# A new written-out order for the first 18 pairs of an attention and feed-forward kernel

## The chip, the cores and the metric

The kernel runs on one core of a Trainium2 chip. The metric is the time of one execution in microseconds (us), as the median of the runs shown. The profile is that of one execution; its span runs from the first to the last instruction of the program, and the execution's own time is a little longer.

Five engines work side by side, each through its own instructions in order: PE (TensorE, matmuls), ACT (ScalarE), DVE (VectorE), POOL (GpSimd) and SP (SyncE, which here only issues DMAs). They wait for each other by semaphores.

## The reference

Cosine attention over 8 batches, 12 heads, 448 positions of 64 numbers, then a feed-forward layer over all 3584 rows:

```python
q_n = q / (norm(q) + 1e-6);  k_n = k / (norm(k) + 1e-6)
attn = softmax(q_n @ k_n.T / tau)               # per head, tau = 0.1
x = (attn @ v).transpose(0, 2, 1, 3).reshape(3584, 768)
h = x @ w_in                                    # 768 x 2048
out = (h * clip(h + 3, 0, 6) / 6) @ w_out       # 2048 x 768
```

## The kernel before, in words

**Pairs and items.** Two heads make a pair; there are 48 pairs, six to a batch. The inputs come as items: item 2d and 2d+1 hold q and k of pairs 2d and 2d+1 (448 KB each; from item 14 on k comes first). Everything is computed in bf16 after the norms. PE does the matmuls of both halves of the work, so attention of later batches runs between the feed-forward units of earlier ones.

**Order by hand.** The instructions of all engines are issued in the order in which the program calls its helper functions. Up to pair 17 this order is a text, `PLAN` (L21 to L58), read word by word by `run` (L960); each word is a function and its arguments. Behind it, a loop over pairs 18 to 47 (L999) has an order of its own. Within one engine the order of the words is the order of execution. The words are:

- `LQ.j` loads item j on SP's queue (L189); it takes over the buffer of item j - 7, so it waits for that item's scaling. `LV.d` loads v of two pairs by four DMAs on SP (L201); its buffer was that of d - 3, so it waits for the casts of that one's two pairs.
- `SQ.j.e.c.n` squares n columns of item j on engine e, which is a (ACT), p (POOL) or v (DVE) (L211). `RE.j` sums the squares on DVE (L228). `NO.d` makes 1/(norm + eps) of items 2d and 2d+1: by four small ACT operations, or, with a `v` behind it, by two of ACT and two of DVE (L246 to L262). `NM.j.e` scales item j by it (L266), on POOL unless `v` is given. Items 0 and 1 are squared, summed and scaled in pieces; a number behind the word says which half.
- `TR.j` transposes item j on PE, seven small matmuls into a PSUM bank (L314); from item 14 on `XD.j` does it by a DMA on SP (L325). `CQ.i`, `CK.i` and `CS.i` copy queries and keys of pair i out of it (L352 to L388).
- `SC.i.g` computes scores of group g (of four) of pair i on PE (L395), `EX.i.g` their exps on ACT (L428). `VC.i.e` casts v of pair i (L285), `VA.i.g` multiplies exps by v on PE, eight small matmuls (L453). Up to pair 5, scores go to two double banks, so a group waits for the exps of the group two before; behind `OPEN` (L926) to a ring of six banks that all PE results share.
- `FI.i` divides by the sums on DVE (L473). `BK.i` transposes the result back on PE and `CX.i` copies it into the input of the feed-forward layer on DVE (L490, L498); `XP` and `XB` do both by DMA.
- `W` asks for the next eighth of the weights, by a DMA on POOL's queue that also casts them to bf16 (L908). Four pieces make w_in: the first two hold its columns 0 to 1023, the next two the rest. Four make w_out.
- `U` runs the next unit of the feed-forward layer on PE. A unit of the first weight matmul is six matmuls of 448 columns (`mm1_unit`, L561, matmuls at L567); it needs `CX` of the batch's six pairs, the weight pieces of its columns, and a bank of the ring. `UA` and `UV` run the ACT and DVE operations that empty a unit's bank (L576, L582). The order has 30 such units (16 of batch 0, 14 of batch 1), then 6 of the second weight matmul of batch 0 (`mm2_unit`, L607, sixteen matmuls each at L614). Later units take sums of blocks so that seven products do for eight (`product_unit`, L721, matmuls at L740).
- `DP.n` runs n fillers of 248 columns on PE, `D.n` n fillers of 512 columns: matmuls of a zero tile whose results nobody reads (L914 to L924).
- `GL` and `WS` copy and add blocks on DVE.

Each helper names what must have been issued ahead of it (`needs`, L167), and the waits between engines follow from the buffers that it reads and writes. For the first unit that is

```python
def mm1_unit(b, fc):
    needs(*(("CX", i) for i in range(b * HP, (b + 1) * HP)))
    assert len(weights) <= 6 - 2 * (2 * fc // FCN)
```

that is, two pieces of the weights must have been asked for ahead of units 1 to 8 of a batch (`fc` 0 to 7), four ahead of units 9 to 16.

Of the kernel before, what the change touches and what calls it, by code (L numbers as in the profile page):

```python
# [18 lines left out]
ORDER = "111111111111111111111111111111222222"  # L19

PLAN = [  # L21
    "LQ.1 DP.5 SQ.1.a.11.3 SQ.1.p.4.3 DP.1 SQ.1.a.0.4 LQ.0 SQ.0.p.8.6 DP.2 DP.4 LQ.3 LQ.2 SQ.1.v.7.4 RE.1.1",
    "SQ.0.a.0.6 RE.1.0 NO.0.1 LQ.5 LQ.4 SQ.0.v.6.2 DP.6 NM.1.p.0 D.10 RE.0.1 DP.3 NM.1.p.1 RE.0.0 DP.8 NO.0.0",
    "SQ.3.a.0.7 LV.0 DP.2 SQ.2.a.0.7 NM.0.p.0 RE.3 RE.2 NM.0.p.1 TR.1.Y DP.2 TR.0.Z CK.0.v DP.4 SQ.4.p.0.7 CQ.0.v",
    "SQ.5.a.0.7 LQ.6 NO.1 LV.1 LQ.7 SC.0.0.0 SC.0.1.1 DP.5 DP.3 CQ.1.v EX.0.0 RE.5 RE.4 NM.3.p SC.0.2.0 CK.1.v DP.3",
    "EX.0.1 DP.3 EX.0.2 NM.2.v DP.3 SC.0.3.1 TR.3.Y LQ.8 NO.2 EX.0.3 DP.3 SC.1.0.0 TR.2.Z EX.1.0 VC.0.v SC.1.1.1 DP.2",
    "EX.1.1 VA.0.0 CK.2.v VC.1.v VC.3.v NM.4.p NM.5.p VA.0.1 LQ.9 SC.1.2.0 SQ.6.a.0.7 LQ.11 DP.5 DP.2 SC.1.3.1 EX.1.2",
    "CQ.2.v LQ.10 LV.2 VA.0.2 VA.0.3 DP.3 SC.2.0.0 DP.2 EX.1.3 CK.3.v SC.2.1.1 EX.2.0 TR.4.Y SC.2.2.0 SQ.7.p.0.7",
    "EX.2.1 RE.6 FI.0 RE.7 LV.3 VA.1.0 SQ.8.p.0.7 SC.2.3.1 CQ.3.v VC.2.v CQ.5.v VA.1.1 EX.2.2 SC.3.0.0 EX.2.3 VA.1.2",
    "NO.3 RE.8 SC.3.1.1 CQ.4.v EX.3.0 DP.2 DP.4 EX.3.1 VA.1.3 TR.5.Z SC.3.2.0 W SQ.9.p.0.7 EX.3.2 FI.1 CK.4.v BK.0.Y",  # L30
    "VA.2.0 SC.3.3.1 RE.9 LV.4 EX.3.3 NO.4 VA.2.1 VA.2.2 VA.2.3 SC.4.0.0 EX.4.0 NM.6.p DP.2 SC.4.1.1 SQ.10.p.0.7 W",
    "SQ.11.p.0.7 EX.4.1 CX.0.v TR.6.Y CK.5.v FI.2 CQ.7.v VA.3.0 BK.2.Z RE.10 SC.4.2.0 EX.4.2 NM.7.p CQ.6.v VA.3.1",
    "SC.4.3.1 DP.2 EX.4.3 CX.2.v SC.5.0.0 RE.11 VA.3.2 EX.5.0 SC.5.1.1 VA.3.3 VC.4.p SC.5.2.0 FI.3 VC.5.p EX.5.1",
    "BK.1.Y TR.7.Z SC.5.3.1 CX.1.v CK.6.v CK.7.v VA.4.0 EX.5.2 DP.2 CS.7.v EX.5.3 BK.3.Y VA.4.1 LQ.12 CS.6.v OPEN",
    "DP.2 CX.3.v NO.5 SC.6.0 VA.4.2 VA.4.3 SC.6.1 SC.6.2 EX.6.0 NM.8.p FI.4 EX.6.1 EX.6.2 SC.6.3 TR.8 BK.4 VA.5.0",
    "CX.4.v VA.5.1 CQ.8.v SC.7.0 VA.5.2 EX.6.3 NM.9.p CQ.9.v VC.6.p VA.5.3 SC.7.1 FI.5 EX.7.0 SC.7.2 TR.9 SC.7.3",
    "NM.10.p CK.8.v VA.6.0 EX.7.1 EX.7.2 VC.8.p CS.8.v W BK.5 SQ.12.p.0.7 LQ.13 VA.6.1 VA.6.2 SC.8.0 EX.7.3 CS.9.v",
    "VA.6.3 CK.9.v DP.1 EX.8.0 CX.5.v SC.8.1 SC.8.2 VC.7.p FI.6 LQ.15 EX.8.1 U UA SQ.13.a.0.7 LV.5 U TR.10 EX.8.2 UA",
    "U RE.13 U SC.8.3 UV UA CQ.10.v VA.7.0 W RE.12 UV CQ.11.a UV UA NO.6 U EX.8.3 VA.7.1 VA.7.2 UV VC.9.p VA.7.3",
    "NM.11.p SC.9.0 FI.7 NM.12.p UA SC.9.1 UV EX.9.0 U VA.8.0 SC.9.2 EX.9.1 VC.10.p UA SC.9.3 TR.11 UV NM.13.p",  # L40
    "CS.11.v XP.6 VA.8.1 LQ.14 EX.9.2 SQ.15.a.0.7 VA.8.2 U EX.9.3 CK.11.v CK.10.v VA.8.3 SC.10.0 TR.12 U CS.10.v FI.8",
    "UA UV VA.9.0 SC.10.1 LQ.17 EX.10.0 SQ.14.p.0.7 CQ.12.v CQ.13.v SC.10.2 UA VA.9.1 LQ.19 VA.9.2 EX.10.1 LQ.16",
    "VA.9.3 LV.6 W UV SC.10.3 EX.10.2 U SC.11.0 FI.9 EX.10.3 SC.11.1 U UA EX.11.0 LV.7 EX.11.1 UV UA SC.11.2 RE.15",
    "BK.8 LQ.18 CX.8.v U VA.10.0 U VA.10.1 UA EX.11.2 UV UV RE.14 SC.11.3 UA BK.9 VA.10.2 VA.10.3 FI.10 EX.11.3 TR.13",
    "NO.7 CK.13.v CS.13.v CX.9.a U UV CK.12.a VC.11.p W VA.11.0 U SC.12.0 CS.12.v VA.11.1 VA.11.2 UA BK.10 VA.11.3 UV",
    "UA NM.15.p UV EX.12.0 CX.10.v SC.12.1 EX.12.1 SC.12.2 FI.11 U EX.12.2 BK.11 SC.12.3 UA NM.14.p SQ.16.p.0.6 U UA",
    "CX.11.v UV U SC.13.0 SQ.17.p.0.7 XD.14 UV RE.17 EX.12.3 VC.12.p EX.13.0 SQ.16.a.6.1 U UA RE.16 VC.15.p U VA.12.0",
    "UV XD.15 UA U UA UA UV SC.13.1 SQ.19.p.0.7 VC.13.p SC.13.2 UV EX.13.1 LQ.21 U VA.12.1 VA.12.2 UA UV RE.19",
    "VA.12.3 EX.13.2 UV NO.8 W U SC.13.3 NM.16.p CK.15.v CK.14.v U UA UA SQ.18.a.0.7 EX.13.3 U SC.14.0 FI.12 UA",
    "VA.13.0 VC.14.p CS.14.v UV VA.13.1 UV EX.14.0 UV U SC.14.1 SC.14.2 VA.13.2 VA.13.3 UA EX.14.1 UV U W SC.14.3",  # L50
    "FI.13 U VA.14.0 NM.17.p UA EX.14.2 UA VA.14.1 EX.14.3 XD.17 U UV VA.14.2 RE.18 SC.15.0 SC.15.1 UA UV EX.15.0 U",
    "XD.16 EX.15.1 UA UV VA.14.3 SC.15.2 U UA SC.15.3 EX.15.2 FI.14 NO.9 LV.8 VA.15.0 LV.9 UV CK.16.v UV EX.15.3 U",
    "SQ.21.p.0.7 VA.15.1 RE.21 CS.16.v LQ.20 SC.16.0 LQ.22 SC.16.1 UA VC.16.p SC.16.2 VC.17.p VA.15.2 EX.16.0 VA.15.3",
    "XP.12 NM.18.v CK.17.v XD.18 U EX.16.1 SQ.20.a.0.7 NM.19.p FI.15 WS.6 U UV XD.19 SC.16.3 RE.20 GL.0 WS.1 WS.7.0",
    "EX.16.2 U VA.16.0 UA VA.16.1 LV.11 EX.16.3 SC.17.0 UV VC.19.p SC.17.1 SC.17.2 SQ.22.v.0.7 VA.16.2 LQ.23 EX.17.0",
    "VA.16.3 EX.17.1 LV.10 U SC.17.3 XP.14 NO.10 FI.16 NM.20.p CK.18.v U CK.19.v WS.7.1 WS.y3 XB.16 EX.17.2 UV UA",
    "VA.17.0 VC.18.p EX.17.3 CS.18.v WS.y4.0",
]  # L58


# [1037 lines left out]
```

## Time and profile before

| | |
|---|---|
| time, median of 3 runs | 406.7 us (406.68 to 407.45) |
| profiled execution | 404.91 us, span 403.1 us |
| clock granted to TensorE | 1.0 throughout |
| instructions | 9619 |
| moved by DMA | 65.32 MB, 162 GB/s on average |
| q or k loads | 48 of 448 KB, 4.4 to 4.9 us from issue to landing (median) |
| weight pieces | 8 of 768 KB, 9.2 to 10.2 us (median) |

How to read it: the page gives each engine's busy time and its share of the span; then the span in 40 slices; the DMA queues; the chain of waits, which follows the work back from the last instruction to whatever released it; and groups of instructions by line, engine and tile, with `out<-in`, the number, the busy time and the mean duration. A timeline has one line for a run of like instructions: start, length, engine, line, operation, tiles, number, and in brackets the idle time ahead of it with what ended it. "Pitch" below is the time from one start to the next of the same engine; it is shorter than an instruction's duration, since they overlap by a tenth of a microsecond or so.

### The profile page before, as it was taken

What the parts mean: (1) busy time and instruction counts of PE and PEld (TensorE: products, weight loads), DVE (VectorE), ACT (ScalarE), POOL (GpSimd) and SP (SyncE); (2) the same over time, 40 slices, a digit from 0 to 9 for tenths busy, and PEclk for the clock granted to TensorE, in tenths of its full rate; (3) what the DMA queues carried; (4) which work ended last, traced back from release to release, by engine and by line L of the source; (5) the groups of instructions that cost most, each with busy time, mean ns of one, the idle gap of its engine ahead of it and who ended that gap; (6) DMA issues with size and microseconds to landing.
All of it is one profiled execution on the core that took longest, in us unless ns stands there. A gap on an engine that the chain in (4) does not pass through costs nothing.

```text
span 403.1 us, 9619 instructions
## 1 busy us (share of the span) xinstructions
PE 395.5 (98%) x3696; PEld 234.3 (58%) x3696; DVE 286.4 (71%) x503; ACT 278.3 (69%) x609; POOL 234.0 (58%) x228
## 2 busy tenths in 40 slices
...
GB/s 289 281 254 257 216 247 230 156 125 230 187 213 220 139 128 228 171 222 130 180 216 212 152 130 164 182 192 145 192 154 76 112 46 67 41 79 21 26 73 99
DMA packets 91566, 65.32 MB, mean 162 GB/s; under 512 B 56064, under 2 KB 89984, under 8 KB 91520
## 3 DMA queue, kind: packets, MB, share of 16 engines
q1 hardware_dynamic: 87408, 58.02, 62.8%
q0 software_dynamic: 3712, 6.29, 9.0%
...
q10 hardware_dynamic: 400, 0.39, 0.3%
...
## 4 chain that ended last, share of the span: by engine, by line
PE 94%; DVE 3%; DMA 1%; ACT 0%; issue 0%; DVEq 0%; ACTq 0%
PE M L567 24%; PE M L740 17%; PE PV L462 13%; PE Y L567 6%; PE M L422 6%; PE Z L567 5%; PE Y L740 4%; PE Z L740 4%; PE M L614 3%; PE M L820 2%; PE Z L422 2%; PE PV L922 2%; PE Z L820 1%; PE Y L422 1%; DVE n L238 1%; PE SC L422 1%
## 5 line engine op out<-in xcount | busy, mean ns | idle before, releaser
L440 ACT ACTIVATE at<-M 128x448 bf16<-128x448 f32 x200 | 99.9, 568 | 16.4 <-PE M L422 14.4
L567 PE MATMUL M<-xT,w_in_sb 128*128 128x448 bf16 x522 | 110.8, 352 | 0.0
L567 PEld LDWEIGHTS <-w_in_sb 128*128 128x128 bf16 x768 | 72.0, 98 | 62.6 <-issue 2.8
L274 POOL TENSOR_TENSOR nrm<-big,r 128x896 bf16<-128x896 f32 (+1 forms) x48 | 79.5, 1662 | 26.1 <-ACT r L262 19.3
L576 ACT ACTIVATE u<-M,bias 128x448 bf16<-128x448 f32 x87 | 57.0, 655 | 25.2 <-PE M L567 24.8
L582 DVE SCALAR_TENSOR_TENSOR gT<-u,M 128x448 bf16<-128x448 bf16 x76 | 46.7, 618 | 36.8 <-ACT u L576 36.3
L226 POOL TENSOR_TENSOR big<-big 128x896 f32<-128x896 f32 (+3 forms) x39 | 63.9, 1641 | 10.9 <-DMA big<-in_k_dram 5.7
L462 PEld LDWEIGHTS <-at 128*128 128x128 bf16 (+1 forms) x1536 | 54.9, 97 | 22.8 <-issue 13.5
L462 PE MATMUL PV<-vx,at 128*128 128x65 bf16 (+1 forms) x1536 | 64.3, 194 | 0.2 <-DVE on L483 0.2
L238 DVE TENSOR_REDUCE n<-big 128x14 f32<-128x896 f32 (+1 forms) x50 | 51.7, 1041 | 5.6 <-ACT big L224 4.6
L379 POOL COPY km<-tT 64x128 bf16<-64x128 bf16 x34 | 12.8, 376 | 58.1 <-DMA tT<-nrm 45.1
L769 POOL TENSOR_TENSOR big<-big 128x384 f32<-128x384 f32 x11 | 11.8, 1076 | 54.6 <-ACT big L788 54.5
L740 PEld LDWEIGHTS <-gT 128*128 128x128 bf16 x288 | 27.8, 98 | 20.0 <-DVE gT L718 0.6
L740 PE MATMUL M<-w_out_sb,gT 128*128 128x384 bf16 x208 | 37.9, 326 | 0.1
L440 ACT ACTIVATE at<-Z 128x448 bf16<-128x448 f32 x49 | 27.7, 565 | 9.9 <-PE M L422 7.3
L483 DVE TENSOR_TENSOR on<-PV,rc 128x512 bf16<-128x512 f32 x48 | 33.2, 691 | 1.7
L293 POOL CAST vx<-big 128x512 bf16<-128x512 f32 x44 | 33.2, 757 | 1.2 <-DMA big<-in_v_dram 1.1
L422 PE MATMUL M<-tT,kz 64*128 64x448 bf16 (+1 forms) x175 | 31.6, 351 | 0.0
L740 PEld LDWEIGHTS <-gs 128*128 128x128 bf16 x224 | 21.5, 98 | 14.8 <-DVE gs L718 0.4
L567 PE MATMUL Y<-xT,w_in_sb 128*128 128x448 bf16 x132 | 28.6, 352 | 0.0
L440 ACT ACTIVATE at<-Y 128x448 bf16<-128x448 f32 x45 | 25.7, 570 | 3.1 <-PE Z L422 1.7
L740 PE MATMUL M<-w_sum,gs 128*128 128x384 bf16 x144 | 26.3, 326 | 0.0
...
## 6 DMA issues: line engine op xcount, KB each, us to landing
...
w_in_sb<-in_moe_w_in_dram POOLq DMA_DIRECT2D x4, 768.0 KB, 10.2
w_out_sb<-in_moe_w_out_dram POOLq DMA_DIRECT2D x4, 768.0 KB, 9.2
tT<-nrm SPq DMA_TRANSPOSE x34, 3.3
xT<-on SPq DMA_TRANSPOSE x25, 3.8
```

What stands on the lines that cost most here:

```text
L226: engines[e].tensor_tensor(out=o, in0=i, in1=i, op=ALU.mult)
L238: nc.vector.tensor_reduce(out=n2s[d % 2][:, j % 2, c], in_=sq[:, :, :, :].rearrange("p g c d -> p (g c) d")[:, c, :], axis=AX.X, op=ALU.add,)
L274: engines[e].tensor_tensor(out=nrm[:, :, g, :].rearrange("p c g d -> p g c d"), in0=raw_of[j][:, g, :, :], in1=rs[d % 2][3][:, j % 2, :] . ...
L293: (engines[e].copy if e == "a" else engines[e].tensor_copy)(out=o, in_=f)
L422: nc.tensor.matmul(o, ks, qt[rows], start=True, stop=True)
L440: nc.scalar.activation(out=o, in_=x, func=AF.Exp, scale=inv_tau)
L462: nc.tensor.matmul(pv_out(j, h), at[rows, n, q_cols(i // HP, j)], vt[rows, 3 + h if name == "M" else 5 * h + int(name[1]), :], start=(name ...
L483: nc.vector.tensor_tensor(out=on[:, :, :, :].rearrange("p j h d -> p h j d"), in0=pv4[:, :, :, 0:D], in1=rc[:, :, :].to_broadcast([128, 2, ...
L567: nc.tensor.matmul(ps[:, 0:S], w_in_sb[:, cc, fc * 128 : (fc + 1) * 128], x[:, cc, 0:S], start=(cc == 0), stop=(cc == CC - 1),)
L576: nc.scalar.activation(out=u[:, :], in_=ps[:, 0:S], func=AF.Relu, bias=half_bias, scale=1.0 / 6.0)
L582: nc.vector.scalar_tensor_tensor(out=g[:, fc, c0 : c0 + S], in0=u[:, :], scalar=1.0, in1=ps[:, 0:S], op0=ALU.min, op1=ALU.mult,)
L740: nc.tensor.matmul(m, lhs[:, c, :], rhs[:, c, c0 : c0 + width], start=(base is None and c == 0), stop=(c == KC - 1), skip_group_check=True,)
```

## The change

Only the text `PLAN` changes: the same operations of pairs 0 to 17 in another order, and some of them on other engines. No function changes, nor does anything behind pair 17.

- Norms 0 (its second half) to 4 and 6 get the `v`: two of their ACT operations are replaced by two on DVE.
- The squares of items 0 and 1 are cut and ordered otherwise (item 0 first, before item 1 first). Of the later ones, items 13, 15, 18 and 20 go from ACT to POOL and items 19, 21 and 5 or 4 change sides; item 22 goes from DVE to ACT.
- Scaling of items 2 and 18 goes from DVE to POOL, casts of v change engine for pairs 0, 6, 16 and 18, and a few copies of queries, keys and results move between ACT and DVE.
- There are 96 fillers of 248 columns in place of 86, and the 10 of 512 columns are gone. 75 of the 96 stand ahead of the first transpose, `TR.0` (before: 31, and the 10).
- The first `W` stands in pair 0, behind the scaling of items 0 and 1 (before: in pair 3); the second follows the scaling of item 6 (before: between the squares of items 10 and 11).
- On DVE, `CX.5` stands ahead of the key copies of pairs 8 and 9 (before: behind them), and `CX.3` ahead of those of pair 7; `RE.10` and `RE.11` stand behind `CX.5` (before: ahead of the results of pair 4).
- The first `U` stands behind `VA.6.3` and `SC.7.2`; before it stood behind `SC.8.2`.
- `LQ.7` stands ahead of `LQ.6`; `LQ.14` and `LV.6` stand ahead of `XP.6` on SP's queue (before: behind it).

The first half of each order:

```diff
@@ PLAN @@
-    "LQ.1 DP.5 SQ.1.a.11.3 SQ.1.p.4.3 DP.1 SQ.1.a.0.4 LQ.0 SQ.0.p.8.6 DP.2 DP.4 LQ.3 LQ.2 SQ.1.v.7.4 RE.1.1",
-    "SQ.0.a.0.6 RE.1.0 NO.0.1 LQ.5 LQ.4 SQ.0.v.6.2 DP.6 NM.1.p.0 D.10 RE.0.1 DP.3 NM.1.p.1 RE.0.0 DP.8 NO.0.0",
-    "SQ.3.a.0.7 LV.0 DP.2 SQ.2.a.0.7 NM.0.p.0 RE.3 RE.2 NM.0.p.1 TR.1.Y DP.2 TR.0.Z CK.0.v DP.4 SQ.4.p.0.7 CQ.0.v",
-    "SQ.5.a.0.7 LQ.6 NO.1 LV.1 LQ.7 SC.0.0.0 SC.0.1.1 DP.5 DP.3 CQ.1.v EX.0.0 RE.5 RE.4 NM.3.p SC.0.2.0 CK.1.v DP.3",
-    "EX.0.1 DP.3 EX.0.2 NM.2.v DP.3 SC.0.3.1 TR.3.Y LQ.8 NO.2 EX.0.3 DP.3 SC.1.0.0 TR.2.Z EX.1.0 VC.0.v SC.1.1.1 DP.2",
-    "EX.1.1 VA.0.0 CK.2.v VC.1.v VC.3.v NM.4.p NM.5.p VA.0.1 LQ.9 SC.1.2.0 SQ.6.a.0.7 LQ.11 DP.5 DP.2 SC.1.3.1 EX.1.2",
-    "CQ.2.v LQ.10 LV.2 VA.0.2 VA.0.3 DP.3 SC.2.0.0 DP.2 EX.1.3 CK.3.v SC.2.1.1 EX.2.0 TR.4.Y SC.2.2.0 SQ.7.p.0.7",
-    "EX.2.1 RE.6 FI.0 RE.7 LV.3 VA.1.0 SQ.8.p.0.7 SC.2.3.1 CQ.3.v VC.2.v CQ.5.v VA.1.1 EX.2.2 SC.3.0.0 EX.2.3 VA.1.2",
-    "NO.3 RE.8 SC.3.1.1 CQ.4.v EX.3.0 DP.2 DP.4 EX.3.1 VA.1.3 TR.5.Z SC.3.2.0 W SQ.9.p.0.7 EX.3.2 FI.1 CK.4.v BK.0.Y",
-    "VA.2.0 SC.3.3.1 RE.9 LV.4 EX.3.3 NO.4 VA.2.1 VA.2.2 VA.2.3 SC.4.0.0 EX.4.0 NM.6.p DP.2 SC.4.1.1 SQ.10.p.0.7 W",
-    "SQ.11.p.0.7 EX.4.1 CX.0.v TR.6.Y CK.5.v FI.2 CQ.7.v VA.3.0 BK.2.Z RE.10 SC.4.2.0 EX.4.2 NM.7.p CQ.6.v VA.3.1",
-    "SC.4.3.1 DP.2 EX.4.3 CX.2.v SC.5.0.0 RE.11 VA.3.2 EX.5.0 SC.5.1.1 VA.3.3 VC.4.p SC.5.2.0 FI.3 VC.5.p EX.5.1",
-    "BK.1.Y TR.7.Z SC.5.3.1 CX.1.v CK.6.v CK.7.v VA.4.0 EX.5.2 DP.2 CS.7.v EX.5.3 BK.3.Y VA.4.1 LQ.12 CS.6.v OPEN",
-    "DP.2 CX.3.v NO.5 SC.6.0 VA.4.2 VA.4.3 SC.6.1 SC.6.2 EX.6.0 NM.8.p FI.4 EX.6.1 EX.6.2 SC.6.3 TR.8 BK.4 VA.5.0",
-    "CX.4.v VA.5.1 CQ.8.v SC.7.0 VA.5.2 EX.6.3 NM.9.p CQ.9.v VC.6.p VA.5.3 SC.7.1 FI.5 EX.7.0 SC.7.2 TR.9 SC.7.3",
-    "NM.10.p CK.8.v VA.6.0 EX.7.1 EX.7.2 VC.8.p CS.8.v W BK.5 SQ.12.p.0.7 LQ.13 VA.6.1 VA.6.2 SC.8.0 EX.7.3 CS.9.v",
-    "VA.6.3 CK.9.v DP.1 EX.8.0 CX.5.v SC.8.1 SC.8.2 VC.7.p FI.6 LQ.15 EX.8.1 U UA SQ.13.a.0.7 LV.5 U TR.10 EX.8.2 UA",
-    "U RE.13 U SC.8.3 UV UA CQ.10.v VA.7.0 W RE.12 UV CQ.11.a UV UA NO.6 U EX.8.3 VA.7.1 VA.7.2 UV VC.9.p VA.7.3",
...
+    "DP.2 DP.1 DP.5 LQ.0 DP.1 DP.10 DP.1 DP.11 DP.16 SQ.0.a.8.6 DP.16 DP.5 SQ.0.a.6.2 LQ.1 SQ.0.p.0.6 LQ.2 RE.0.0",
+    "RE.0.1 SQ.1.a.0.4 LQ.3 DP.7 SQ.1.a.4.3 SQ.1.p.7.4 LQ.4 SQ.1.v.11.3 LQ.5 RE.1.0 NO.0.0 NM.0.p.1 LV.0 LV.1 RE.1.1",
+    "NM.0.p.0 NO.0.1.v TR.0.Y SQ.2.a.0.7 SQ.3.a.0.7 LQ.7 RE.2 LQ.6 NM.1.p.0 RE.3 SQ.4.a.0.7 NM.1.p.1 TR.1.Z CK.0.v",
+    "CQ.0.a DP.4 SC.0.0.0 SC.0.1.1 W CQ.1.v NO.1.v EX.0.0 DP.8 SC.0.2.0 CK.1.v RE.4 SQ.5.p.0.7 RE.5 VC.0.p NM.2.p",
+    "VC.1.v EX.0.1 EX.0.2 DP.4 SC.0.3.1 VA.0.0 VC.3.v EX.0.3 VA.0.1 SC.1.0.0 VA.0.2 SC.1.1.1 TR.2.Y VA.0.3 NM.3.p",
+    "NO.2.v EX.1.0 SC.1.2.0 VC.2.v TR.3.Z EX.1.1 SQ.7.p.0.7 CQ.2.v NM.4.p NM.5.p SC.1.3.1 FI.0 EX.1.2 LQ.8 EX.1.3",
+    "CQ.3.v CK.2.v DP.1 VA.1.0 VA.1.1 SQ.6.a.0.7 CK.3.v SC.2.0.0 LQ.9 LV.2 SC.2.1.1 EX.2.0 LQ.11 VA.1.2 EX.2.1 VA.1.3",
+    "BK.0.Y DP.3 SC.2.2.0 LV.3 RE.7 SQ.9.p.0.7 TR.4.Z SC.2.3.1 FI.1 RE.6 CQ.4.v EX.2.2 VA.2.0 CX.0.v VA.2.1 CQ.5.v",
+    "SC.3.0.0 VA.2.2 EX.2.3 VA.2.3 NO.3.v FI.2 EX.3.0 SC.3.1.1 SQ.8.p.0.7 TR.5.Y SC.3.2.0 EX.3.1 EX.3.2 VA.3.0 NM.6.p",
+    "CK.4.v BK.1.Z SC.3.3.1 EX.3.3 RE.9 CX.1.v VA.3.1 SC.4.0.0 VC.4.p CK.5.v VA.3.2 SC.4.1.1 LQ.12 VA.3.3 RE.8 EX.4.0",
+    "FI.3 EX.4.1 VC.6.v BK.2.Z SC.4.2.0 TR.6.Y SC.4.3.1 LQ.10 VA.4.0 CQ.7.v EX.4.2 EX.4.3 CQ.6.v CX.2.v LV.4 W NM.7.p",
+    "VA.4.1 SC.5.0.0 VA.4.2 NO.4.v VA.4.3 SC.5.1.1 EX.5.0 FI.4 VC.5.p TR.7.Y EX.5.1 CS.6.v NM.8.p CK.6.v SC.5.2.0",
+    "BK.3.Z VC.7.p VA.5.0 LQ.15 SC.5.3.1 EX.5.2 EX.5.3 CX.3.v VA.5.1 OPEN SC.6.0 CK.7.v LV.5 EX.6.0 VA.5.2 VA.5.3",
+    "CS.7.v FI.5 SC.6.1 SC.6.2 DP.1 EX.6.1 BK.4 TR.8 W EX.6.2 LQ.13 SC.6.3 EX.6.3 CX.4.v VC.9.p CQ.8.v VA.6.0 BK.5",
+    "SQ.10.p.0.7 VA.6.1 CQ.9.v SC.7.0 SC.7.1 EX.7.0 EX.7.1 CX.5.v SC.7.2 NM.9.p VC.8.p RE.10 VA.6.2 VA.6.3 U EX.7.2",
+    "SC.7.3 FI.6 LQ.14 TR.9 CK.8.v LV.6 U UA U UA CS.8.v UV EX.7.3 CK.9.v CS.9.v SQ.11.p.0.7 UA UV SC.8.0 RE.11 UV",
+    "EX.8.0 W NO.5 SQ.12.p.0.7 SC.8.1 VA.7.0 VA.7.1 VA.7.2 EX.8.1 VC.10.p RE.12 VA.7.3 U U SC.8.2 SQ.13.p.0.7 UA UA",
+    "NM.10.p EX.8.2 U SC.8.3 FI.7 VC.11.p UA NM.11.p UV EX.8.3 UV W TR.10 CQ.11.v SC.9.0 LQ.17 U UV VA.8.0 CQ.10.a",
+    "EX.9.0 SQ.14.p.0.7 SC.9.1 SC.9.2 TR.11 VA.8.1 RE.13 VA.8.2 UA UV NO.6.v SC.9.3 VA.8.3 EX.9.1 XP.6 U RE.14 LQ.18",
+    "FI.8 U NM.12.p EX.9.2 UA EX.9.3 SQ.15.p.0.7 CK.10.a CS.11.v CK.11.v U VA.9.0 UV CS.10.v UA SC.10.0 UV UA SC.10.1",
...
```

## The prediction

> **What bounds the kernel now.** I read the busy table and the 40 slices first, then the chain of waits, then the windows, then the timelines of PE, ACT and POOL up to 50 us.
>
> ```profile
> PE 395.5 (98%) x3696; PEld 234.3 (58%) x3696; DVE 286.4 (71%) x503; ACT 278.3 (69%) x609; POOL 234.0 (58%) x228
> ...
> PE 94%; DVE 3%; DMA 1%; ACT 0%; issue 0%; DVEq 0%; ACTq 0%
> ```
>
> TensorE is the bound, with 94% of the chain. A busy PE isn't always a useful one, so I split it by stage, with the windows (columns: stretch, its length, busy us and count of PE, weight load, DVE, ACT, POOL, then clock, DMA share, GB/s):
>
> ```profile
> 12.50:42.90 30.40, 29.96 (x422) 19.59 (x422) 26.16 (x61) 29.14 (x59) 29.06 (x24) 1.00 1.07 263
> 42.90:80.00 37.10, 37.10 (x373) 21.23 (x373) 26.72 (x55) 32.95 (x72) 21.07 (x20) 1.00 1.05 214
> 80.00:115.50 35.50, 35.50 (x343) 21.16 (x341) 28.33 (x41) 25.41 (x59) 16.75 (x15) 1.00 0.90 181
> ```
>
> In the first of them ACT, POOL and DMA are as full as PE, and 49 of PE's matmuls are fillers on a zero tile (L922). The PE timeline shows where that stage starts and ends:
>
> ```profile
> 2.48 3.90 PE L922 MATMUL PV<-xT 128*128 128x248 bf16 x18 [2.48 <-DVE vx L975]
> 6.17 2.78 PE L917 MATMUL Y<-xT 128*128 128x512 bf16 x10
> 8.79 1.54 PE L922 MATMUL PV<-xT 128*128 128x248 bf16 x13
> ...
> 12.47 0.55 PE L422 MATMUL SC<-tT,kz 64*128 64x448 bf16 x4 [0.65 <-DVE tT L341]
> ...
> 42.85 2.43 PE L567 MATMUL M<-xT,w_in_sb 128*128 128x448 bf16 x12
> ```
>
> The first scores run at 12.47, the first unit of the first weight matmul at 42.85, and the written-out order ends (first scores of pair 18, L422) at 115.49. From 42.85 on PE has no hole. I counted the order of before in steady pitches read from that stretch (unit of six 1.135 us, second-matmul unit 2.60, eight value matmuls 0.245, a score pair 0.19, seven transposes 0.39, four 0.22, and 0.095 for each change between 64 and 128 rows): 72.3 us against 72.64 measured, so 0.34 us of waits. All that follows pair 18 is the same code. So the time is that of **the first unit** plus the PE work behind it, and the change is priced by what it does to both.
>
> **The PE work behind the first unit.** In the new order the first unit stands one pair earlier: four score groups and one set of transposes fewer are ahead of it (22.07 us of real work instead of 23.31, same pitches). Behind it stand 73.64 instead of 72.3. With the same 0.34 of waits that is 73.98, 1.34 more. The change gains if the first unit starts before 42.85 - 1.34 = 41.5.
>
> **The start.** The new order puts 75 fillers ahead of the first transposes (before: 31 of 248 columns and 10 of 512). They start at 2.48 again, after the same memsets. In the timeline the first 18 take 207 ns each, the clock doubles at 7.03 (single starts in the trace), then they take 106. So 22 run cold up to 7.03, and 53 warm ones take 5.6 us: TR.0 starts at 12.65 and TR.1 ends at 13.6 (0.39 + 0.39 + 0.16). The data would be ready sooner: squares, reduction, norms and scaling of items 0 and 1, in the rows of before (loads land at 4.29 and 5.49, reductions 0.54, scaling 0.90 each), end at 9.4 and 11.3. So the fillers are on the path here. CK.0 on DVE (0.38) and the hop give first scores at 14.15, first exp at 14.55 (before 12.87): 1.7 us later. The Trainium skill, page "TensorE: Matmul & The Clock Gate", section "Part 1: The HAM clock gate", gives about 3.4 us of work to warm up, where this trace shows 4.55; by that rule the fillers would end at 12.1.
>
> **The early weights.** The first piece is issued on POOL behind the scaling of item 1, at 11.3 instead of 23.07. The page's queue table prices it:
>
> ```profile
> q1 hardware_dynamic: 87408, 58.02, 62.8%
> q0 software_dynamic: 3712, 6.29, 9.0%
> ```
>
> Queue 0 carries only the eight weight pieces: 9.0% of 403.1 us over 8 is 4.5 us of all DMA engines each. A q or k load takes 1.2 us (the first five land at 4.29, 5.49, 6.70, 7.90, 9.11), the four transfers of a v load 2.1. DMA is full in this stage, so a piece issued early pushes loads. LV.0 lands at 12.82 as before; behind it stand LV.1, LQ.7 and LQ.6: without weights LQ.6 lands at 12.82 + 2.1 + 1.2 + 1.2 = 17.3, with the whole piece ahead of it at 21.8. When both queues had work (33 to 39 us) their packets alternated one for one, so nearly all 464 packets of the piece pass before LQ.6; I take 22.0. ACT gets to SQ.6 at 14.55 + 6.2 = 20.75 (two pairs of exps at 3 x 0.80 + 0.44, and 0.53 of norms), so it waits 1.25; queued behind it are all exps of pair 2, and PE's scores of pair 2 from the third group on wait for their banks. Before, LQ.6 landed at 14.18 and nobody waited. The late start is thus partly hidden by this wait, not added to it.
>
> The Trainium skill, page "DMA: Bandwidth & Descriptors", section "Anatomy of one DMA — SWDGE (gpsimd) path", has 2.0 us plus bytes over 436 GB/s: an estimate of 3.8 us for the 786 KB. The trace has 7.3 to 14.4. By the page's figure LQ.6 would not be waited for, which is the fast rival below.
>
> **ACT to the first unit.** Pair 2's exps start at 22.0 + 0.84 = 22.85 (before 21.05). Up to the first half exp of pair 7, which frees the first unit's PSUM bank: four pairs at 2.84, two norms at 0.53, pair 6 as seven at 0.42, one of 0.54: 15.9. That is 38.75. The same stretch took 18.7 before; the new one is shorter because norms 0 to 4 end on DVE, which takes two of four ACT operations (0.35 + 0.13, with some waiting 0.55) off ACT per norm. Their DVE twins (28 columns) don't occur in the trace; the nearest rows are a 59 ns memset and a 0.21 us reciprocal of 8 columns, so 0.1 to 0.5 us for both; I take 0.4. DVE can bear that: its sum from CK.0 brings FI.5 at 36.5 and, because the copies of pair 8's and 9's keys now stand behind it, CX.5 at 38.6 (before, CX.5 ended at 42.31 behind six such copies). PE's own work from 14.15, fillers included, is 23.4: 37.6, so PE doesn't set it. With 0.3 for scores of pair 6 behind CK.6, the first unit could go at 39.1.
>
> It also needs the second weight piece. POOL issues it behind SQ.7 (whose load lands near 20.7) and 10.4 us of squares, scaling and one cast (1.63, 1.65, 0.56 each): at 31.1. Pieces took these times:
>
> ```profile
> w_in_sb<-in_moe_w_in_dram POOLq DMA_DIRECT2D x4, 768.0 KB, 10.2
> w_out_sb<-in_moe_w_out_dram POOLq DMA_DIRECT2D x4, 768.0 KB, 9.2
> ```
>
> At 7.3 (the fastest) it lands at 38.4, at 14.4 at 45.5. I take 8, since the load queue is then briefly empty (LQ.15 waits for NM.8 until 36): **39.2, first unit 39.4**. If the piece is later, SC.7.3, TR.9 and all units behind the first one stand still on PE with it, and nothing else fills the hole. That alone is 39.4 + 73.98 = 113.4, 2.1 us before 115.49.
>
> **The fourth piece.** Unit 9 reads the other half of w_in. It stands 14.7 us behind the first unit (before 15.7): 54.1 against 58.6. All loads and pieces up to it cost DMA 38.9 us (9 q/k loads at 1.2, five v loads at 2.1, four pieces at 4.5 or a little less); from 12.82 that took until 53.33 before, 1.6 us of it idle. In the new order LQ.14 and LV.6 (3.3 us) stand ahead of the transpose XP.6 instead of behind it and share the engines: 53.3 to 56.6. I take 54.7, a wait of 0.6. Later the sums leave room: the last w_out piece is issued at about 84 and read at 95; ACT has 56.8 us of work in the 74 behind the first unit.
>
> **Sum.** -(42.85 - 39.4) + 1.34 + 0.6 = -1.5 us. The profiled execution takes 404.9 (span 403.1 and 1.8 around it): 403.4. The median of the runs shown is 406.7, 1.8 above that execution; the forecast in its terms is **405.2**.
>
> **Rivals.** *Loads aren't held up* (the weights yield): ACT at 20.75 doesn't wait, the first unit goes at 37.7 by PE's and ACT's sums, unit 9 finds its weights: -3.8, 402.9. For it: the first piece took 9.8 us to land in before without anybody waiting. Against it: DMA is full.
>
> *The first unit waits for its second weights* (the slow side): place, w_in's second piece behind POOL's squares; price, landing 41.5 to 45.6; from 41.5 on it costs more than the order gains. At the middle, 43.5, the plan ends at 117.5: +2.0, 408.7. For it: in before this piece took 13.7 and landed at 42.55, just ahead of the first unit. Against it: 4 of those us were spent behind the first piece.
>
> *Unit 9 waits for the fourth piece to the last load*: 56.6 + 59.3 of PE work is 115.9: +0.4, 407.1, no measurable change; so much for the change not doing what it says: an earlier start that is given back at once.
>
> *The clock falls back.* Only 17 fillers remain behind the first scores (before 49). The Trainium skill, page "TensorE: Matmul & The Clock Gate", section "Part 1: The HAM clock gate", has the clock halved after some 3.4 us of idle PE. In rows: two stretches of 4.5 us at 207 instead of 106 ns per filler cost 4.5 us: +3.0, 409.7. Against it: PE's 23.4 us of work fill 93% of its 25.
>
> **Chances.** Forecast 0.42 (its own range 404.1 to 406.0), no hold-up 0.12, second weights 0.26, unit 9 0.15, clock 0.05. A measurement here can tell about 0.2% (0.8 us) from no change. Faster 0.52, same 0.17, slower 0.31. The range 402.8 to 409.0 leaves out half of the fast rival, the upper part of the second-weights one and the clock.
>
> **What the changed profile would show.** PE: 75 fillers from 2.48 to about 12.7, first scores near 14.1. ACT: a wait of about 1 us for in_q_dram ahead of SQ.6 near 21. PE: first L567 near 39.4, unit 9 near 54.7, first scores of pair 18 near 114. If the first L567 stands later than 41.5, or a hole of over 2 us opens ahead of any later unit, the prediction is wrong.

## The result and the profile after

The changed kernel takes **417.2 us** (median of 6 runs, 415.05 to 419.58) against 406.4 for the kernel before on the same chip: ratio 1.027, 95% interval 1.0245 to 1.0303. 405.2 was forecast, 402.8 to 409.0 the range. It is slower by about 11 us, outside the range. All ratios here and below leave out runs over 1.5% above the fastest run of their kernel: none of these two kernels, but one of 4 of e3 (417.8 us), two of 9 of e4, two of 4 of e7, two of 6 of e9, one of 6 each of e10 and e11, and one of 5 of e8 (2246 us).

The profiled execution took 419.6 us, with a span of 417.7. These are its busy table, its granted clock in 40 slices, and its chain of waits:

```profile
PE 398.5 (95%) x3696; PEld 237.3 (57%) x3696; DVE 283.8 (68%) x511; ACT 275.7 (66%) x598; POOL 238.8 (57%) x231
...
PEclk9999969999899999999999999999999999999999
...
PE 79%; DMA 9%; SPq 4%; DVE 3%; POOL 2%; ACT 2%; issue 1%; POOLq 0%; DVEq 0%
```

PE's share of the chain fell from 94 to 79%, DMA's rose from 1 to 9%, and SP's queue, which was not in it, has 4%. The clock, full before, has two dents. The windows of the changed kernel (stretch, length, busy us and count of PE, weight load, DVE, ACT, POOL, then clock, DMA share, GB/s) show where; I cut them at the first unit (41.29), unit 9 (63.57), the last unit of the first weight matmul (102.98) and 113.00, where the clock is full again:

```profile
12.68:41.29 28.61, 25.68 (x395) 17.36 (x393) 24.55 (x60) 24.55 (x43) 24.57 (x20) 1.00 1.11 258
41.29:63.57 22.28, 17.70 (x154) 9.72 (x151) 12.76 (x27) 13.91 (x33) 15.89 (x14) 0.85 1.06 232
63.57:102.98 39.41, 38.80 (x392) 21.89 (x391) 26.71 (x56) 34.48 (x74) 21.16 (x20) 1.00 0.87 171
102.98:113.00 10.02, 6.06 (x39) 3.44 (x37) 6.50 (x8) 3.82 (x10) 5.99 (x5) 0.83 0.51 93
```

In the second and the fourth of them PE isn't busy throughout and its clock is at 0.85 and 0.83. PE's own list of waits (engine, line and tile, what it waited for; us in total, times, longest) names the two:

```profile
PE M L318 <- POOL nrm L273: 4.6, 1, 4.6
PE M L613 <- DVE gT L581: 4.0, 1, 4.0
PE PV L921 <- DVE vx L974: 2.5, 1, 2.5
```

(The third is the wait for the memsets ahead of the first filler, as before. Lines are one lower than in the kernel before, since `PLAN` is a line shorter.)

**Hole 1: `TR.10` waits for `NM.10`.** PE's timeline:

```profile
50.65 0.35 PE L421 MATMUL M<-tT,kz 128*128 128x448 bf16 x1
55.59 0.93 PE L318 MATMUL M<-ident,nrm 128*128 128x128 bf16 x7 [4.58 <-POOL nrm L273]
...
56.93 2.42 PE L566 MATMUL M<-xT,w_in_sb 128*128 128x448 bf16 x6
```

The unit at 56.93 takes 2.42 for six matmuls where 1.3 is usual: the clock is at half from 54.92 for 6.83 us. POOL's timeline shows why the scaling is late:

```profile
49.30 0.61 POOL L292 CAST vx<-big 128x512 bf16<-128x512 f32 x1 [3.01 <-PE Y L566]
52.21 1.68 POOL L225 TENSOR_TENSOR big<-big 128x896 f32<-128x896 f32 x1 [2.29 <-DMA big<-in_k_dram]
53.84 1.69 POOL L273 TENSOR_TENSOR nrm<-big,r 128x896 bf16<-128x896 f32 x1
```

The third line is `NM.10`. Ahead of it POOL stands at `VC.10` and at `SQ.13`. The profile puts the first stop down to a matmul, but the last transfer of `LV.5` lands at 49.16, just ahead of 49.30; the second is for `LQ.13`, landed at 52.07. Those loads were asked for at 36.5 to 40.1 and took 9 to 12 us, beside the third and fourth weight pieces (36.56 to 48.21 and 43.90 to 56.60). That these two pieces are what slows them is argued from the times; no run moved them away. Before, `LQ.13` was asked for at 29.1 and landed at 42.0, and `NM.10` ran at 37.8, ahead of all this on POOL.

**Hole 2: unit 31 waits for a bank.** PE, then DVE:

```profile
102.98 1.30 PE L566 MATMUL Z<-xT,w_in_sb 128*128 128x448 bf16 x6
108.23 4.05 PE L613 MATMUL M<-w_out_sb,gT 128*128 128x384 bf16 x16 [3.96 <-DVE gT L581]
```

```profile
100.73 0.62 DVE L581 SCALAR_TENSOR_TENSOR gT<-u,Z 128x448 bf16<-128x448 bf16 x1 [0.80 <-ACT u L575]
106.46 0.35 DVE L368 COPY kz<-tT 128x384 bf16<-128x384 bf16 x1 [5.11 <-DMA tT<-nrm]
...
107.57 0.61 DVE L581 SCALAR_TENSOR_TENSOR gT<-u,M 128x448 bf16<-128x448 bf16 x1
```

The bank is freed by the product at 107.57, which stands in DVE's order behind `CK.16`, a copy of keys that waits 5.11 us for the transpose `XD.16`. SP's queue:

```profile
95.31 1.44 SPq L519 DMA_TRANSPOSE xT<-on  x1
96.85 7.01 SPq L329 DMA_TRANSPOSE tT<-nrm  x2
```

The order there is `XP.12` (which waits for `FI.13`), `XD.17`, `XD.16`; issued at 95.31, 96.85 and 100.13, they land at 104.7, 105.6 and 106.4, behind the eighth weight piece (94.74 to 102.28). Before, both `XD` stood ahead of `XP.12` (88.3 and 89.7, landed at 94.0 and 96.5). The clock is at half from 109.53 for 3.41 us.

**The account**, in spans: first unit 41.29 instead of 42.85, -1.56; the longer order behind it, +1.34; stalls behind it, 129.71 - 41.29 - 73.98 = +14.44; behind pair 18, +0.36. Together 14.58, which is 417.72 - 403.14. Of the stalls the two waits are 4.58 + 3.96 = 8.54, and 10.24 us at half clock cost up to 5.12.

### The profile page after: what moved, and what is told of

The parts are those of the page before. It is cut to its first block, busy times and chain, and to the rows that moved or that the text cites. A ratio compares the mean times of both kernels' runs of the same rounds, so it can differ in the third digit from the quotient of the medians.

```text
span 417.7 us, 9622 instructions
## 1 busy us (share of the span) xinstructions
PE 398.5 (95%) x3696; PEld 237.3 (57%) x3696; DVE 283.8 (68%) x511; ACT 275.7 (66%) x598; POOL 238.8 (57%) x231
## 4 chain that ended last, share of the span: by engine, by line
PE 79%; DMA 9%; SPq 4%; DVE 3%; POOL 2%; ACT 2%; issue 1%; POOLq 0%; DVEq 0%
PE M L566 20%; PE M L739 16%; PE PV L461 10%; PE Y L566 5%; PE Z L566 5%; PE M L421 5%; DMA big<-in_k_dram 5%; PE Y L739 4%; PE Z L739 3%; PE M L613 3%; DMA big<-in_q_dram 2%; PE M L819 2%; SPq L329 2%; PE Z L819 1%; PE Z L421 1%; SPq L208 1%
## 5 line engine op out<-in xcount | busy, mean ns | idle before, releaser
L439 ACT ACTIVATE at<-M 128x448 bf16<-128x448 f32 x199 | 98.9, 562 | 18.6 <-PE M L421 16.3
L566 PE MATMUL M<-xT,w_in_sb 128*128 128x448 bf16 x498 | 106.4, 355 | 0.0
L273 POOL TENSOR_TENSOR nrm<-big,r 128x896 bf16<-128x896 f32 (+1 forms) x50 | 82.1, 1646 | 22.8 <-ACT r L261 13.4
L225 POOL TENSOR_TENSOR big<-big 128x896 f32<-128x896 f32 (+4 forms) x42 | 67.6, 1611 | 15.0 <-DMA big<-in_q_dram 6.9
L575 ACT ACTIVATE u<-M,bias 128x448 bf16<-128x448 f32 x83 | 54.4, 656 | 27.0 <-PE M L566 26.5
L581 DVE SCALAR_TENSOR_TENSOR gT<-u,M 128x448 bf16<-128x448 bf16 x72 | 44.1, 618 | 33.5 <-ACT u L575 32.9
L378 POOL COPY km<-tT 64x128 bf16<-64x128 bf16 x34 | 14.3, 420 | 62.3 <-DMA tT<-nrm 31.7
L292 POOL CAST vx<-big 128x512 bf16<-128x512 f32 x42 | 30.2, 719 | 5.5 <-PE Y L566 3.0
L566 PE MATMUL Y<-xT,w_in_sb 128*128 128x448 bf16 x144 | 31.2, 352 | 0.0
L739 PEld LDWEIGHTS <-gs 128*128 128x128 bf16 x224 | 21.6, 98 | 14.5
L566 PE MATMUL Z<-xT,w_in_sb 128*128 128x448 bf16 x126 | 27.3, 352 | 0.0
```

The lines of the kernel that those rows point to most:

```text
L225: engines[e].tensor_tensor(out=o, in0=i, in1=i, op=ALU.mult)
L273: engines[e].tensor_tensor(out=nrm[:, :, g, :].rearrange("p c g d -> p g c d"), in0=raw_of[j][:, g, :, :], in1=rs[d % 2][3][:, j % 2, :] . ...
L292: (engines[e].copy if e == "a" else engines[e].tensor_copy)(out=o, in_=f)
L439: nc.scalar.activation(out=o, in_=x, func=AF.Exp, scale=inv_tau)
L566: nc.tensor.matmul(ps[:, 0:S], w_in_sb[:, cc, fc * 128 : (fc + 1) * 128], x[:, cc, 0:S], start=(cc == 0), stop=(cc == CC - 1),)
L575: nc.scalar.activation(out=u[:, :], in_=ps[:, 0:S], func=AF.Relu, bias=half_bias, scale=1.0 / 6.0)
```

## The experiments

Four theories were tested in turn: the two holes are the whole loss; each is a matter of an engine's order, or of loads that share the DMA engines with a weight piece; the start is bound by the early piece; the early piece is what the order lives on. Ratios are to the kernel before, measured on the same chip.

| kernel | ratio, 95% | span profiled | first unit | pair 18 |
|---|---|---|---|---|
| before | 1 | 403.1 | 42.85 | 115.5 |
| changed | 1.027 (1.0245-1.0303) | 417.7 | 41.29 | 129.7 |
| e1 scaling 10, 11 first | 1.039 (1.0335-1.0445) | 419.4 | 45.61 | 131.5 |
| e2 fillers in the holes | 1.039 (1.0318-1.0457) | 418.2 | 40.90 | 129.7 |
| e3 key transposes first | 1.007 (1.0042-1.0095) | 406.6 | 41.50 | 118.7 |
| e4 = e1 + e3 | 1.0085 (1.0054-1.0116) | 407.8 | 41.69 | 120.0 |
| e5 before, early piece | 1.0055 (1.0025-1.0085) | 406.3 | 46.04 | 118.7 |
| e6 last piece early | 1.024 (1.0193-1.0286) | 416.7 | 45.12 | 129.0 |
| e7 four moves | 1.0155 (1.0101-1.0209) | 409.3 | 42.28 | 121.8 |
| e8 = e3, fewer fillers | 1.009 (1.0054-1.0133) | 408.3 | 42.00 | 119.8 |
| e9 = e3, first piece later | 1.013 (1.0080-1.0177) | 407.5 | 41.42 | 119.6 |
| e10 = e3, scaling 10 first | 1.012 (1.0078-1.0165) | 406.2 | 41.45 | 118.1 |
| e11 = e10, pieces moved | 1.020 (1.0168-1.0233) | 413.2 | 46.17 | 124.9 |
| e12 = e3, first piece at 23 | 1.020 (1.0167-1.0231) | 411.6 | 43.15 | 124.2 |

The intervals come from several runs, the other columns from one. Runs of one kernel of the new order scatter by 3 to 10 us (the one of 2246 us aside), those of before by 2 to 3, so a profile here can be a good or a bad one of its kernel, and the interval decides: the changed kernel's profile is its slowest run, e3's, e7's and e10's are their fastest.

### Hole 1 by POOL's order (e1)

```diff
-EX.8.1 VC.10.p RE.12
+EX.8.1 NM.10.p NM.11.p VC.10.p RE.12
...
-NM.10.p EX.8.2
+EX.8.2
-UA NM.11.p UV
+UA UV
```

> The new order with one thing moved: on POOL the scaling of items 10 and 11 stands ahead of the cast of pair 10 and the squares of item 13 instead of behind them. Theory: PE's hole ahead of TR.10 (4.6 us) is POOL standing at the cast and at SQ.13, whose loads (LV.5, LQ.13) share the DMA engines with the third and fourth weight pieces, and the half clock from 54.9 to 61.8 follows from the hole. Then TR.10 starts near 51 instead of 55.6, the clock stays full there, and the time falls by 4.6 + 3.4 = 8 us to about 409, the second hole (ahead of the first unit of the second weight matmul) staying. Rival: PE would be held up by the late loads or weights anyway; the hole only moves to a later operation and the time stays within 2 us of 417.

The hole at `TR.10` is gone and nothing is won: 3.9% slower than before. In the profiled run the first loads came late (see the last section), so the first unit stood at 45.61 instead of 41.29. From there to the last unit of the first weight matmul it took 56.7 us instead of 61.7, so 5.0 of the 8 us expected were won there, if hole 1 would have been as large in this run. And hole 2 is as large as ever:

```profile
102.34 1.30 PE L566 MATMUL Z<-xT,w_in_sb 128*128 128x448 bf16 x6
108.32 5.28 PE L613 MATMUL M<-w_out_sb,gT 128*128 128x384 bf16 x16 [4.68 <-DVE gT L581]
```

With the late start PE comes to hole 2 only 0.64 us earlier than in the changed kernel. `XP.12` is issued at 94.7 and `XD.16` lands at 106.5, much as there (95.3 and 106.4), and the unit stands at 108.32 (108.23); the half clock lasts 6.83 us instead of 3.41. The profile shows one execution: why all four runs (418.99 to 423.98) were slower than the changed kernel's median is not shown.

### The clock alone (e2)

```diff
-UV W TR.10
+UV W DP.40 TR.10
...
-CS.16.v U U EX.15.2
+CS.16.v U DP.35 U EX.15.2
```

> The new order with 40 more fillers ahead of TR.10 and 35 ahead of unit 31, 4.2 and 3.7 us of PE work at full clock, which stand in the two holes and end before what PE waits for there. Theory of the clock (the halves of clock from 54.9 to 61.8 and 109.5 to 113.0 are paid because PE stood still): clock 1.0 throughout, holes as before, time lower by half of 10.2 us against the profiled run and by 2 to 5 against the median: 412 to 415. Rival (the clock falls for another reason, or its half rate is hidden by waits): 417 or a little more.

At hole 1 the clock stayed full and unit 9 stood at 61.0 instead of 63.57. But this is no test of the clock there: PE came to the fillers at 51.54 and `NM.10` was done at 53.25, so that in this profile the hole would have been 1.7 us, and the 40 fillers, 4.40 us long, put the rest on the path. At hole 2 they didn't help, since the fillers too wait for a bank; they ran behind the hole, and part of the time at half clock:

```profile
104.58 5.41 PE L921 MATMUL PV<-xT 128*128 128x248 bf16 x35 [2.87 <-DVE on L482]
```

The clock fell where PE stood still, here as in the changed kernel; the last section has this for all runs. That PE kept busy would keep the clock is not shown by e2. The 2.6 us by which unit 9 came earlier did reach hole 2: `XP.12` was issued at 92.7 instead of 95.3, `XD.16` landed at 103.2 instead of 106.4, and `CK.16` ran at 103.33 instead of 106.46. But the 35 fillers, 5.41 us long, stood behind the hole, and unit 31 at 109.82. The total (1.039) missed both numbers, and by more than this profile (418.2) shows.

### Hole 2 by SP's order (e3), and both (e4)

```diff
-FI.13 XP.12 RE.19
+FI.13 XD.17 XD.16 XP.12 RE.19
-SQ.21.a.0.7 XD.17 UA
+SQ.21.a.0.7 UA
-EX.15.1 XD.16 UA
+EX.15.1 UA
```

> The new order with XD.17 and XD.16 ahead of XP.12 on SP's queue instead of behind it. Theory: the second hole (5.2 us at unit 30 to 31, then 1.2 of half clock) is DVE standing at CK.16 for the transpose XD.16, which lands at 106.4 because SP waits at XP.12 until FI.13 and that transpose takes 9 us beside the last weight piece; behind CK.16 stand the DVE operations that free the banks of units 28 to 30. Then XD.16 lands several us earlier, the hole shrinks below 1.5 us, and the time falls by 4 to 6 us to 411 to 413. Rival: the last weight piece alone keeps the transposes from landing, whatever their order: within 1.5 us of 417.

1.007 instead of 1.027: 8.3 us less. Not all of it need be the place of the two DMAs, as the profile shows. SP's queue of e3:

```profile
85.23 5.08 SPq L329 DMA_TRANSPOSE tT<-nrm  x2
90.41 1.45 SPq L519 DMA_TRANSPOSE xT<-on  x1
```

`XD.17` lands at 88.3, 3.1 us after it is issued. `XD.16` is issued at 89.1, beside the eighth piece (89.0 to 96.96), and lands with it at 97.0. That is in time: unit 31 waits 0.3. PE's wait at hole 1 was smaller too in this profile, and no clock fell:

```profile
PE M L318 <- POOL nrm L273: 1.4, 1, 1.4
...
PE M L613 <- DVE gT L581: 0.3, 1, 0.3
```

`LQ.13` landed at 49.1 and not at 52.1. The edit is hardly why: in every queue the moved words stand behind all that hole 1 waits for, they are issued 33 us later, and e2, without the edit, would have waited 1.7 us there. Of the 11.0 us by which pair 18 stands earlier than in the changed kernel's profile, 5.3 lie behind the last unit of the first weight matmul (hole 2 and its clock, within the 4 to 6 expected) and 5.9 between the first unit and unit 9 (hole 1 and its clock). How the 8.3 us of the medians divide is not shown.

> The new order with both moves (scaling of 10 and 11 ahead on POOL; XD.17 and XD.16 ahead of XP.12 on SP). Theory: the two holes and their half clock are all that makes the new order slower: 417 - 8 - 5 = 404, at or a little below the kernel before (406.4). Rival: something that the holes hide, such as the fourth weight piece that lands at 56.6, takes their place: 408 or more.

1.0085, no better than e3: the theory's 404 fell. Hole 1 is gone there as well, but waits of 0.7 to 1.5 us stand ahead of `TR.9`, `SC.9.3` and others, and the first scores of pair 18 stand at 120.0, 1.3 behind e3's.

### Hole 2: the order, or the weight piece beside it (e6)

```diff
-SC.13.2 SQ.18.p.0.7
+SC.13.2 W SQ.18.p.0.7
...
-UV W CK.16.v
+UV CK.16.v
```

> The changed kernel, with the eighth weight piece alone moved forward on POOL, ahead of SQ.18, so that it is asked for at about 79 us and not at 94.7; the order on SP is left as it is (XP.12 ahead of XD.17 and XD.16). Theory (the transposes are late because they share the DMA engines with the eighth piece): XD.16 lands 3 to 4 us after it is issued, CK.16 runs by 101, the second hole is mostly gone, 409 to 412 us. Rival (they are late because they stand behind XP.12's wait for FI.13 on SP): the hole keeps its place, 415 to 417 us.

SP's order is the changed kernel's, but the piece is out of the way (82.69 to 93.79):

```profile
98.97 1.28 SPq L519 DMA_TRANSPOSE xT<-on  x1
100.35 2.59 SPq L329 DMA_TRANSPOSE tT<-nrm  x2
```

The three land at 102.7, 103.6 and 104.4, in 3.8, 3.3 and 2.7 us where they took 9.4, 8.7 and 6.2. Unit 31 doesn't wait, the clock stays full there. So the mechanism is the theory's: the transposes are late beside the weight piece, and in time without it. The time is not: 1.024, hardly faster than the change. Behind the first unit the profile is 4.5 us shorter (83.9 instead of 88.4), but the first unit stood 3.8 later (late first loads again), hole 1 is there unchanged (4.5), and the earlier `W` pushes `km` copies and transposes of pair 14 on POOL and DMA, 1.6 us of new waits. Either remedy closes hole 2; moving the transposes was the cheaper one.

### All moves together (e7)

e1, e3, e6, and `LQ.13` earlier:

```diff
-LV.4 W NM.7.p
+LV.4 LQ.13 W NM.7.p
...
-EX.6.2 LQ.13 SC.6.3
+EX.6.2 SC.6.3
```

> The changed kernel with four moves: NM.10 and NM.11 ahead of VC.10 and SQ.13 on POOL, LQ.13 asked for ahead of LQ.15 and of the second weight piece, XD.17 and XD.16 ahead of XP.12 on SP, and the eighth weight piece ahead of SQ.18. Theory (the two holes and the clock that they cost are the whole loss): both are gone, the units follow each other as before from a first unit at about 41.5, and the time is 405 to 406 us, level with the kernel before. Rival (behind each hole there stands another operand that is only just in time, so the waits move on): 408 to 410 us, as with the first two moves together.

The rival, and worse: 1.0155. In its profile both holes are gone, and behind them PE waits for what the moves delayed:

```profile
PE M L421 <- DVE gT L581: 2.6, 2, 1.9
...
PE Y L421 <- POOL km L378: 1.4, 1, 1.4
...
PE M L566 <- DMA w_in_sb<-in_moe_w_in_dram: 0.8, 1, 0.8
```

The last is the first unit, held until 42.28 by the second piece, which landed at 42.15 (41.04 in the changed kernel) with `LQ.13` asked for beside it.

### What bounds the start (e8, e9)

e3 without two of the filler entries ahead of `TR.0`:

```diff
-DP.11 DP.16 SQ.0.a.8.6 DP.16 DP.5
+DP.11 SQ.0.a.8.6 DP.5
```

> The changed kernel with XD.17 and XD.16 ahead of XP.12 on SP (408.9 us when run alone), and two of the three filler entries ahead of the first transposes taken out, so that 43 fillers and not 75 stand there. Theory (by then the start is bound by the first weight piece, LQ.6 behind it and the second piece, not by the fillers): within 1 us of 408.9. Rival (the fillers still stand on the path): 1.6 to 2 us faster, about 407.

1.009 against e3's 1.007, no gain. The transposes start at 9.76 instead of 12.68 and the first exps at 12.60 instead of 14.5, but `LQ.6` lands at 22.2, as in the changed kernel, and there the lead is gone; ACT waits 2.6 us for it instead of 1.7:

```profile
22.22 0.95 ACT L223 ACTIVATE big<-big 128x896 f32<-128x896 f32 x1 [2.62 <-DMA big<-in_q_dram]
```

Next, e3 with the first piece one POOL operation later, behind `LQ.7` and `LQ.6`:

```diff
-SC.0.1.1 W CQ.1.v
+SC.0.1.1 CQ.1.v
...
-SQ.5.p.0.7 RE.5
+SQ.5.p.0.7 W RE.5
```

> The changed kernel with XD.17 and XD.16 ahead of XP.12 on SP (408.9 us by itself), and the first weight piece asked for one POOL operation later, behind SQ.5 (about 12.9 us and not 11.0), when LQ.7 and LQ.6 are already in SP's queue. Theory (the piece stands ahead of LQ.6 and holds it back to 22): LQ.6 lands at 17 to 19, ACT's wait of 1.6 us ahead of SQ.6 goes, the first unit stands at 39.8 to 41, held by the second piece's landing at worst, and the time is 407 to 408.5 us. Rival (the two queues share the engines from then on whichever stands first): LQ.6 lands within 1 us of 22, no change.

`LQ.6` lands at 19.0, ACT's wait is gone and the exps of pair 2 start at 21.4 instead of 22.9, as the theory has it. The first unit doesn't move: 41.42, and 1.013 misses the theory's 407 to 408.5 us. The wait has gone to POOL:

```profile
26.05 3.32 POOL L225 TENSOR_TENSOR big<-big 128x896 f32<-128x896 f32 x2 [2.95 <-DVE r L258]
29.32 1.69 POOL L273 TENSOR_TENSOR nrm<-big,r 128x896 bf16<-128x896 f32 x1
```

The operation named as the releaser was long done: POOL's first squares there are those of item 9, whose load lands at 25.9 (25.5 in e3, asked for at 16.5); behind them stands `NM.6`, for which `TR.6` waits 1.1 us on PE. Three things end within a microsecond of one another: ACT's exps, POOL's scaling and the second piece (40.7). With the DMA engines at 1.11 of their time from 12.68 to 41.29, taking one load ahead puts another back.

### Hole 1 by the smallest move (e10), and the weights (e11)

e3, and on POOL only `NM.10` ahead of `SQ.13`:

```diff
-SC.8.2 SQ.13.p.0.7 UA UA NM.10.p
+SC.8.2 NM.10.p SQ.13.p.0.7 UA UA
```

> The changed kernel with XD.17 and XD.16 ahead of XP.12 on SP (408.9 us by itself), and on POOL NM.10 ahead of SQ.13 (which waits for LQ.13), VC.10 left ahead of both. Theory (hole 1 is POOL's order: NM.10 needs nothing that is late): NM.10 starts as soon as VC.10 is done, about 1.7 us earlier, the wait of TR.10 goes, 407 to 408 us. Rival (something behind it on POOL is then late by as much, SQ.13 and the scaling of items 11 to 13): no change, 408.5 to 409.5.

In the profile it does what it should: `NM.10` starts at 49.0, and no wait at `TR.10` is left; the plan ends at 118.1, the best of the new order. The runs say otherwise: 1.012, not told apart from e3.

e11 also has the first piece of e9 and the second behind `NM.5`:

```diff
-NM.5.p SC.1.3.1
+NM.5.p W SC.1.3.1
...
-LV.4 W NM.7.p
+LV.4 NM.7.p
```

> The changed kernel with all of: XD.17 and XD.16 ahead of XP.12, NM.10 ahead of SQ.13, the first weight piece behind SQ.5, and the second one behind the scaling of item 5, in POOL's wait for LQ.9 (about 23 us and not 31). Theory (the weight pieces' places decide, each by what it shares the DMA engines with): the second piece lands by 34 to 38 and no longer bounds the first unit, which stands at 39.5 to 40.5; behind it the order runs with under 2 us of waits, 404.5 to 406.5 us, level with the kernel before or a little better. Rival (the piece at 23 holds back LQ.8 to LQ.11 and LV.2, on which the scaling and the value products of pairs 2 to 4 wait): a hole ahead of the first unit, which stands at 42 or later, 409 us or more.

The rival: 1.020, first unit at 46.17. The second piece lands at 34.9, 6 us earlier, but `LV.4`, asked for at 27.9 to 32.3, lands at 38.6 to 40.2 and `LQ.10` at 38.4; DVE's and POOL's work stands behind them. DVE:

```profile
35.37 0.69 DVE L290 TENSOR_REDUCE vx<-big 128x512 bf16<-128x512 f32 x1 [3.30 <-DMA big<-in_v_dram]
```

### The early piece by itself (e5, e12)

In the kernel before:

```diff
-RE.2 NM.0.p.1 TR.1.Y
+RE.2 NM.0.p.1 W TR.1.Y
...
-SC.3.2.0 W SQ.9.p.0.7
+SC.3.2.0 SQ.9.p.0.7
```

> The kernel before, with the first piece of w_in asked for in pair 0 (behind NM.0.p.1) in place of pair 3, and nothing else of the new order. Theory (the loss sits in the order behind the first unit, not in the early piece): the early piece takes DMA time from loads that have slack in that order, so the time stays within 2 us of 406.4. Rival (the early piece alone holds the loads of pairs 2 to 6 back, and with them all that follows): 410 us or more.

1.0055: 2 us slower, just at the theory's bound. `LV.1` lands at 21.2 instead of 16.2 and `LQ.9` at 24.6 instead of 21.0, the first unit at 46.04 instead of 42.85; behind it the order runs as before, 72.6 us. The third load landed late in this profile already (7.5 instead of 6.7), ahead of the piece, so part of this can be chance. The early piece alone gave no earlier start, and made no hole behind the first unit.

Undone in the new order (e3 with the first `W` behind `NM.5`):

```diff
-SC.0.1.1 W CQ.1.v
+SC.0.1.1 CQ.1.v
...
-NM.5.p SC.1.3.1
+NM.5.p W SC.1.3.1
```

> The changed kernel with XD.17 and XD.16 ahead of XP.12 on SP (408.9 us by itself), and the early first weight piece undone: it is asked for behind the scaling of item 5, at about 23 us or earlier, as it was before (23.07), and the second piece keeps its place. Theory (the DMA engines bound this stage, and the piece asked for at 11 takes the time of the loads behind it, LQ.6 to LQ.9, on which ACT's squares and POOL's scaling of item 6 wait): LQ.6 lands by 18 and LQ.9 by 22 instead of 25.5, POOL's wait of 2.6 us ahead of SQ.9 shrinks to under 1, and the second piece is issued near 29; then the pieces bound the first unit, which stands at 41 to 43, so that the time is 408 to 410 us: the early piece won nothing and cost little. Rival (the early piece is what brings the first unit forward): the first unit falls back to 44 or later, 411 us or more.

1.020, slower than e3: by its time the rival is right, by its first unit (43.15) neither quite. `LQ.9` lands at 24.4, so POOL's wait ahead of `SQ.9` is gone; but now `LV.4` shares the engines with both pieces and its last transfer lands at 43.8 (37.5 in e3). POOL:

```profile
44.33 0.62 POOL L292 CAST vx<-big 128x512 bf16<-128x512 f32 x1 [5.37 <-DMA big<-in_v_dram]
44.90 1.69 POOL L225 TENSOR_TENSOR big<-big 128x896 f32<-128x896 f32 x1
46.55 1.69 POOL L273 TENSOR_TENSOR nrm<-big,r 128x896 bf16<-128x896 f32 x1
```

It is hole 1 once more, one item earlier: a cast waits for a v load, squares and `NM.9` stand behind it, and PE waits 3.7 us at `TR.9`. So asking for the piece later gained nothing in this order. (The first loads were late in this profile too, so some of it may be chance.)

## Why the prediction was wrong

**The step that failed** is "with the same 0.34 of waits that is 73.98". The PE work behind the first unit was counted rightly and taken to run without holes because it did so before. It measured 88.4: 14.4 us of stalls. The sentence that was to cover it, "Later the sums leave room", compared each engine's work with the time it has. Sums can't see an order: POOL and DVE had room, but stood still in front of a late operand while work that PE needed queued behind. Of the moves past SP's queue the prediction looked at `LQ.14`, `LV.6` and `XP.6`, not at `XP.12`, `XD.17` and `XD.16`, nor at `NM.10` behind `VC.10` and `SQ.13` on POOL. e3's profile puts hole 2 with its clock at 5.3 us, and e3 and e6 show its cause: key transposes queued behind `XP.12`, beside a weight piece. e1 and e10, in which `TR.10` doesn't wait, show that hole 1 is POOL's order; it was 5.9 us longer in the changed kernel's profile than in e3's, where the order on POOL is the same, so its size varies from run to run with the landing of `LV.5` and `LQ.13`. Of the 11 us of the medians e3 won back 8.3; what part of these is which hole stays open.

**The start** was right: fillers end at 12.68 (12.65 predicted), first scores 14.11 (14.15), first exp 14.51 (14.55), `LQ.6` at 22.41 (22.0), ACT's wait 1.72 (1.25). The Trainium skill, page "DMA: Bandwidth & Descriptors", section "Anatomy of one DMA — SWDGE (gpsimd) path", has a fit that gives an estimate of 3.8 us for a piece; here the eight took 7.5 to 12.7, so the trace was the better guide.

**The first unit** was mis-sized by 1.9 us: 41.29 instead of 39.4. Its forecast was the second piece's landing at 8 us; it took 10.2 (30.85 to 41.04), which alone would have moved the unit to about 41.2. PE did not wait for it, since ACT was as late. ACT's stretch from `EX.2.0` to the end of the first half exp of pair 7 took 17.8 instead of 15.9 and ended at 41.06. 1.1 us of that are three waits for scores that the sum left out. ACT's timeline in the changed kernel has two of them:

```profile
36.80 0.98 ACT L439 ACTIVATE at<-M 128x448 bf16<-128x448 f32 x2 [0.43 <-PE M L421]
...
40.51 1.85 ACT L439 ACTIVATE at<-M 128x448 bf16<-128x448 f32 x4 [0.46 <-PE M L421]
```

At 41.29 the first unit sat at the break-even of 41.5 that the prediction had worked out, so even without holes there would have been next to nothing to win (0.2 us); in e9, e11 and e12 no other place of the pieces that was tried brought it forward.

**Rivals.** The second-weights rival named one of the two late suppliers, but not its price: the piece landed just under its point of 41.5. "Unit 9 waits for the fourth piece to the last load" had that piece at 56.6, and it landed at 56.60, but unit 9 had by then been overtaken by hole 1 (63.57). The clock did fall back, in this profile not at the start, of which the rival spoke, but as a sequel of the holes (in those of e1, e6 and e8 it fell at 23.6 to 25.4 us as well). The test set at the end, "a hole of over 2 us opens ahead of any later unit", was met twice.

**What stays open.** With hole 2 closed (e3) the profile is 3.5 us longer than before: -1.35 for the first unit, +1.34 of order, +3.2 of small waits behind it, +0.3 at the end. No version of the new order beat the kernel before. Why its runs scatter, and with them hole 1, is not settled; the profiles give one execution each.
